# Turning uncentred x and taking its mean off in PSUM, loading q and w2 in smaller parts, and moving the side work to later slots

## The chip, the cores and the metric

Each run uses one core of one Trainium2 chip; the experiments were spread over four chips, each with runs of the kernel before in its own rounds. The metric is the device time of an execution in microseconds (us), the median of several. The kernel before takes 290.69 us (three runs, 290.58 to 290.82). All runs in this study count as fast; there is no slow run among them to set aside. Their mean granted clock of PE still differs a little: nine single executions have 0.991 to 0.994 (one each of e1, e3, e9, e11 and e17, two each of e5 and e12), all others 0.997 or more. Those nine are the slowest of their kernels, by 1.0 to 3.0 us over the mean of the others. What makes the clock dip is not shown; in e5's trace it reads 0.73 from 95 to 100 us, around the end of PE's longest wait there (2.06 us, over at 96.68).

Engines are named as in the profile: PE is TensorE, ACT is ScalarE, DVE is VectorE, POOL is GpSimd; PEld is PE's loading of weights, SP is SyncE. PSUM is the memory in which this kernel accumulates PE's products, SBUF the one in which it keeps its other tiles.

## The reference, cut to what matters

```python
kv  = einsum('bhsd,bhse->bhde', k, v)               # B=8, H=8, S=576, D=64
o   = einsum('bhsd,bhde->bhse', q, kv)
x   = o / sqrt(mean(o*o, -1) + 1e-6) * g_norm       # then [B, S, 512]
xn  = (x - mean(x)) / sqrt(var(x) + 1e-6) * g_ln
out = x + relu(xn @ w1) @ w2                        # 512 -> 2048 -> 512
```

## The kernel before

The rows are worked on in 36 tiles of 128 rows: four per batch, and one tile of remainders for each pair of batches. All large products are bf16 matmuls on PE. Their order is fixed: the w1 matmuls of batch 0, its w2 matmuls, w1 of batch 1, and so on. "mm1" and "mm2" below are those two products.

Everything else (k^T v, q times kv, norms, transposes) is side work that has to be ready before the w1 matmuls of its batch. It is woven into the stream by an agenda. A slot is one w1 group (16 matmuls of 128 columns in batches 0 and 1) or four w2 matmuls. Slots 0 to 15 are w1 of batch 0, 16 to 31 its w2, 32 to 47 w1 of batch 1 (four slots for each tile), and so on. When the program is built, everything registered for a slot is emitted just before that slot's matmuls:

```python
def at(slot, fn): agenda.setdefault(int(slot), []).append((slot, fn))
def tick():
    for _, fn in sorted(agenda.pop(clock[0], []), key=lambda e: e[0]): fn()
    clock[0] += 1

def plan_tile(s, make, turn_at, on_pe):
    at(s, first)           # o on PE; square on ACT; reduction on DVE
    at(s + 2, second)      # root on ACT; inverse, y, x, centred xc on DVE
    at(s + 6, third)       # variance on ACT
    at(turn_at, fourth)    # xc^T: on PE with an ACT copy, or by DMA
```

So a slot number does not delay an instruction in time. It decides where it stands in each engine's queue, and each engine works its queue off in order (e12 below shows it for DVE). The slots that the change moves:

```python
at(20, lambda: (rstd_of(0), t.clear()))
at(14.5, q_start); at(19, q_turns); at(22, lambda: kv_of(1))
for j, s, tn in ((0, 24, 30), (1, 27, 34), (2, 31, 38), (3, 35, 42)):
    plan_tile(s, lambda j=j: main_tile(1, j), tn, True)
at(36, lambda: kv_of(2))
at(36.9, lambda: turn_q_dma(2))      # DVE repacks q of batch 2, then a DMA transposes it
for j, s, tn in ((0, 45, 51), (1, 49, 55), (2, 53, 61), (3, 57.5, 64)):
    plan_tile(s, lambda j=j: main_tile(2, j), tn, False)
# ... likewise for batches 3 to 7 and the remainders
```

The start is done by hand. For batch 0's first tiles, x is formed on DVE in f32, then centred and multiplied by g_ln in two halves, each half transposed on PE and copied to SBUF:

```python
t[0].x_g()                           # x = (o * g_norm) * inv, f32, with its row sum
for c, xc in enumerate(halves_xc(0)):            # xc = (x - mean) * g_ln, bf16, 256 columns
    half_turn(0, c, xc, nc.scalar.copy)          # 2 transposes, 1 copy 128x256
t[1].red(); t[1].x_g()
xc1 = list(halves_xc(1))
# slot 1: the rest of q's turns, turn of tile 1, o of tile 2;  slot 2: x of tile 2
# slot 5: turn of tile 2, o of tile 3
```

mm2 of batch 0 keeps four PSUM accumulators open and runs through w2's rows in three parts, `(0, 8), (8, 12)` for all four tiles, then `12 to 16` tile by tile, each followed by its closing step `finish` on DVE (scale, add x, store).

## Time and profile before

| | before |
|---|---|
| median | 290.69 us (290.58 to 290.82) |
| profiled span | 288.8 us |
| PE busy | 280.9 us, 97% |
| DVE, ACT busy | 149.8 and 153.2 us, 52% and 53% |

From the page of the kernel before, the engine table (busy time, share of the span, instructions) and the row that gives PE's busy share in 40 equal slices, in tenths:

```profile
PE 280.9 (97%) x2295; PEld 157.9 (55%) x2295; DVE 149.8 (52%) x331; ACT 153.2 (53%) x333; POOL 41.0 (14%) x69
PE   7889999999999999999999999999999999999994
```

PE bounds it. Only the first slices have air. The view of waits of the kernel before, for PE (what was waited for: us in total, times, longest), says the same; it leaves out very short waits:

```profile
PE even L225 <- DMA v_in<-in_v_dram: 1.5, 1, 1.5
PE p L198 <- DVE eps_sb L137: 1.2, 1, 1.2
PE tp L554 <- DVE xc L547: 0.4, 1, 0.4
PE p L413 <- DMA xT_blk<-xc: 0.2, 1, 0.2
```

The first two are at the very start (loads of k and v; the first fill matmuls, which do no useful work and are meant to warm PE up). The third is the wait for tile 1's centred x, at 17.30 us. The last is one wait near 112 us. In between, for 95 us, the view has no wait of PE.

The timeline of the kernel before, 14 to 20 us, all engines (start us, us, engine, line, operation, out<-in, count, in brackets the idle time before and its releaser). L554 are the transposes of tiles 0 and 1, L413 the w1 matmuls:

```profile
14.20 0.68 PE L554 MATMUL tp<-identity,xc 128*128 128x128 bf16 x4
14.52 0.77 ACT L555 COPY xT_blk<-tp 128x256 bf16<-128x256 bf16 x2 [1.10 <-PE tp L554]
14.95 1.34 PE L413 MATMUL p<-xT_blk,w_sb 128*128 128x128 bf16 x16
...
17.30 0.29 PE L554 MATMUL tp<-identity,xc 128*128 128x128 bf16 x2 [0.39 <-DVE xc L547]
...
18.05 1.26 PE L413 MATMUL p<-xT_blk,w_sb 128*128 128x128 bf16 x16
```

Tile 0's first w1 group starts at 14.95, tile 1's at 18.05. This stretch is what the change wants to shorten. Now a stretch in the middle, w1 of batch 1, in the same view (PE lines, one DVE line and one POOL line):

```profile
53.96 1.96 PE L413 MATMUL p<-xT_blk,w_sb 128*128 128x128 bf16 x32
55.45 0.82 DVE L203 COPY q_p<-q_in 128x2560 bf16<-128x2560 bf16 x1
55.76 0.39 PE L348 MATMUL tp<-identity,xc 128*128 128x128 bf16 x4
55.98 3.74 PE L413 MATMUL p<-xT_blk,w_sb 128*128 128x128 bf16 x64
...
61.72 0.68 POOL L93 DMA_DIRECT2D k_in<-in_k_dram  x1 [0.31 <-issue]
```

The turn of a tile at 55.76 and 64 w1 matmuls behind it, without a gap. DVE repacks q of batch 2 at 55.45, and when its DMA transpose has landed, POOL may issue the loads of batch 3, at 61.72.

### The profile page before, as it was taken

The page shows a single profiled execution, that of the slowest core. Times are in us where ns is not written, and L with a number is a line of the kernel's source. Part 1 is how long each engine was busy: PE and PEld are TensorE (multiplying, and loading weights), DVE is VectorE, ACT ScalarE, POOL GpSimd, SP SyncE. Part 2 cuts the span into 40 slices and gives each one's busy share as a digit, 9 for nine tenths or more (in the row PEclk, how much of TensorE's full clock was granted, in tenths as well). Part 3 has the DMA queues.
Part 4 walks back from the last instruction along what each step waited for, and adds up shares of the span by engine and source line. Part 5 has one row for each costly group of instructions (what it writes and reads, how often), then busy time and mean ns, then how long its engine had stood idle before and what let it go on. Part 6 is the DMA issues. An engine that isn't in the chain of part 4 may idle for free.

```text
span 288.8 us, 5753 instructions
## 1 busy us (share of the span) xinstructions
PE 280.9 (97%) x2295; PEld 157.9 (55%) x2295; DVE 149.8 (52%) x331; ACT 153.2 (53%) x333; POOL 41.0 (14%) x69
## 2 busy tenths in 40 slices
PE   7889999999999999999999999999999999999994
PEld 3579756995479644444444444444444444444444
DVE  5774119938897783764376935762578200220022
ACT  3477844985379733872288318921893066016400
POOL 8522510041005004100500032000000000000000
PEclk9999999999999999999999999999999999999999
DMA  7999999979788959996994189947203410230033
GB/s 214 199 206 205 198 190 195 214 112 193 138 173 101 194 108 157 202 159 120 157 217 68 39 152 219 155 84 149 56 18 64 101 36 0 48 81 19 0 73 75
DMA packets 67546, 36.76 MB, mean 127 GB/s; under 512 B 35516, under 2 KB 62524, under 8 KB 67520
## 3 DMA queue, kind: packets, MB, share of 16 engines
q0 software_dynamic: 28528, 17.76, 43.8%
q1 hardware_dynamic: 38480, 17.91, 31.2%
q10 hardware_dynamic: 512, 0.72, 0.7%
q8 instruction: 18, 0.29, 0.4%
q14 instruction: 8, 0.07, 0.1%
HBM read 36.71 MB, written 9.44 MB: 160 GB/s over the span
## 4 chain that ended last, share of the span: by engine, by line
PE 85%; DMA 5%; DVE 5%; ACT 2%; issue 1%; SPq 1%; DVEq 0%; POOLq 0%
PE p L413 41%; PE p L429 37%; PE o_ps L271 2%; DMA v_in<-in_v_dram 2%; DMA qt<-q_p 2%; PE kv_ps L246 2%; DMA xT_blk<-xc 1%; DVE ss L298 1%; ACT m L416 1%; DVE x_blk L322 1%; DVE y L303 1%; DVE o_sb L434 1%; PE p L198 1%; SPq L205 1%; ACT rms L308 0%
## 5 line engine op out<-in xcount | busy, mean ns | idle before, releaser
L413 PE MATMUL p<-xT_blk,w_sb 128*128 128x128 bf16 (+2 forms) x1024 | 131.6, 286 | 0.6 <-DMA xT_blk<-xc 0.2
L429 PE MATMUL p<-w_sb,m 128*128 128x512 bf16 (+2 forms) x608 | 129.1, 368 | 0.0
L416 ACT ACTIVATE m<-p 128x512 bf16<-128x512 f32 x144 | 85.2, 596 | 43.0 <-PE p L413 40.5
L413 PEld LDWEIGHTS <-w_sb 128*128 128x128 bf16 x1024 | 78.7, 98 | 44.9 <-issue 1.5
L429 PEld LDWEIGHTS <-m 128*128 128x128 bf16 x608 | 57.0, 98 | 62.0
L434 DVE SCALAR_TENSOR_TENSOR o_sb<-p,rstd,x_blk 128x512 f32<-128x512 f32 (+2 forms) x38 | 27.3, 720 | 52.2 <-PE p L429 41.2
L277 ACT ACTIVATE sq<-o_ps 128x512 f32<-128x512 f32 x35 | 20.9, 596 | 41.7 <-PE o_ps L271 41.7
L298 DVE TENSOR_REDUCE ss<-sq 128x8 f32<-128x512 f32 x35 | 23.7, 678 | 13.0 <-ACT sq L277 12.9
L340 ACT ACTIVATE dev<-x_blk,st_blk 128x512 f32<-128x512 f32 x36 | 25.7, 714 | 6.2 <-DVE st_blk L326 6.1
L332 DVE SCALAR_TENSOR_TENSOR xc<-x_blk,st_blk,g_ln_sb 128x512 bf16<-128x512 f32 x34 | 25.6, 752 | 1.2
L303 DVE TENSOR_TENSOR y<-o_ps,inv 128x512 f32<-128x512 f32 x33 | 22.8, 692 | 3.4 <-PE p L413 0.5
L322 DVE SCALAR_TENSOR_TENSOR x_blk<-y,g_norm_sb 128x512 f32<-128x512 f32 x33 | 22.8, 692 | 1.1
L315 DVE RECIPROCAL inv<-rms 128x8 f32<-128x8 f32 x36 | 7.2, 201 | 23.0 <-ACT rms L308 23.0
L422 DVE RECIPROCAL rstd<-rstd 128x4 f32<-128x4 f32 x9 | 1.6, 175 | 31.2 <-ACT rstd L421 31.1
L308 ACT ACTIVATE rms<-ss,eps_sb 128x8 f32<-128x8 f32 x36 | 10.7, 296 | 11.5 <-DVE ss L298 11.4
L98 POOL COPY gate<-qt 1x1 bf16<-1x1 bf16 x5 | 0.9, 177 | 106.4 <-DMA qt<-q_p 106.4
L271 PEld LDWEIGHTS <-qt 128*128 128x128 bf16 (+1 forms) x156 | 10.2, 100 | 8.1 <-issue 1.7
L271 PE MATMUL o_ps<-kv_pack,qt 128*128 128x128 bf16 (+1 forms) x156 | 13.7, 220 | 0.2
L198 PE MATMUL p<-fill_sb 128*128 128x512 bf16 x27 | 8.0, 448 | 1.2 <-DVE eps_sb L137 1.2
L340 ACT ACTIVATION_READ_ACCUMULATOR dev<-x_blk,st_blk 128x1 f32 x36 | 6.8, 189 | 0.0
L249 ACT CAST kv_pack<-kv_ps 64x256 bf16<-64x256 f32 x7 | 2.6, 366 | 7.7 <-PE kv_ps L246 7.7
L246 PEld LDWEIGHTS <-k_in 128*64 128x64 bf16 x280 | 5.0, 112 | 2.6 <-issue 2.5
(80 smaller groups left out, 110.5 us busy)
## 6 DMA issues: line engine op xcount, KB each, us to landing
out_dram<-o_sb SPq DMA_DIRECT2D x70, 128.0 KB, 2.4
w_sb<-in_moe_w_ch_dram POOLq DMA_DIRECT2D x8, 512.0 KB, 15.2
q_in<-in_q_dram POOLq DMA_DIRECT2D x7, 320.0 KB, 12.3
k_in<-in_k_dram POOLq DMA_DIRECT2D x7, 320.0 KB, 6.0
v_in<-in_v_dram POOLq DMA_DIRECT2D x7, 320.0 KB, 8.6
q_in<-in_q_dram POOLq DMA_DIRECT2D x8, 256.0 KB, 12.3
k_in<-in_k_dram POOLq DMA_DIRECT2D x7, 256.0 KB, 6.7
v_in<-in_v_dram POOLq DMA_DIRECT2D x7, 256.0 KB, 10.6
```

The source lines that it names most:

```text
L198: nc.tensor.matmul(p1, lhsT=fill_sb[:, :128], rhs=fill_sb, start=True, stop=True)
L271: nc.tensor.matmul(flat[rows, hp * 128:(hp + 1) * 128], lhsT=lhsT_of(hp), rhs=kvp[:, hp, :], start=True, stop=True)
L277: nc.scalar.activation(self.sq_t, self.o_ps, func=AF.Square)
L298: nc.vector.tensor_reduce(self.ss, self.sq_t, axis=AX.X, op=ALU.add)
L303: nc.vector.tensor_mul(self.y_t, self.o_ps, self.inv().to_broadcast([128, H, D]))
L322: nc.vector.scalar_tensor_tensor(x_blk[:, ts].rearrange("p (h d) -> p h d", h=H), in0=self.y_t, scalar=1.0, in1=g_norm_sb.to_broadcast([12 ...
L332: nc.vector.scalar_tensor_tensor(self.xc_t, in0=x_blk[:, self.ts], scalar=st[:, 1, self.ts:self.ts + 1], in1=g_ln_sb, op0=ALU.add, op1=ALU ...
L340: nc.scalar.activation(dev, x_blk[:, ts], func=AF.Square, bias=st[:, 1, ts:ts + 1], accum_out=st[:, 2, ts:ts + 1])
L413: nc.tensor.matmul(p1[:, i, :], lhsT=w1_sb[:, kk, de * 128:(de + 1) * 128], rhs=blk[2][:, kk, sl], start=(kk == 0), stop=(kk == nK - 1))
L416: nc.scalar.activation(m1[:, de0:de0 + per, sl], p1, func=AF.Relu)
L429: nc.tensor.matmul(p2[:, c0:c1], lhsT=m1s[b][:, de, ts * 128:(ts + 1) * 128], rhs=w2_sb[:, de, c0:c1], start=(de == 0), stop=(de == nDe - 1))
L434: nc.vector.scalar_tensor_tensor(o_sb[:, c0:c1], in0=p2[:, c0:c1], scalar=rstds[b][:, ts:ts + 1], in1=blks[b][0][:, ts, c0:c1], op0=ALU.mu ...
```

## The change

The intent is to feed PE sooner at the start, then to fit the later work to the new pace. It has three parts:

- **A, the start.** For tiles 0 to 2, x is turned without being centred: x^T is a matmul with the identity, and into the same PSUM accumulator goes ones x diag(-mean), which takes the mean off. g_ln is now a factor per partition, applied in the copies out of PSUM, so it is needed transposed; four small fp32 matmuls make it. The f32 x is formed later. q's upper half is loaded in two parts. Tile 2's o and turn get new slots (2 and 4).
- **W, w2.** Its later quarters are loaded in pieces of two row blocks and used as `(0,8), (8,10), (10,12), (12,14)`, then `14 to 16` tile by tile with the closing steps.
- **S, the slots.** Side work of batches 0 to 4 goes to later slots, mostly by one to two. S1 is the tiles of batch 1, S2 is kv and q of batch 2, S34 is the rest.

```diff
+    def x_b(self):                     # A: x without g_ln, not centred, bf16, with its row sum
+        self.i = self.inv().to_broadcast([128, H, D])
+        ...scalar_tensor_tensor(self.xb, in0=self.og_ps, ..., in1=self.i, accum_out=st[:, 0, ts])
+    def mean_b(self):                  # diag = identity * rowsum * (-1/512)
+    def turn_b(self, split):
+        def turned(kk):  matmul(tps[kk // 2][:, kk % 2], lhsT=xb[kk], rhs=identity, start=True, stop=False)
+        def centred(kk): matmul(tps[kk // 2][:, kk % 2], lhsT=ones_sb, rhs=diag, start=False, stop=True)
+        for kk in range(2 if split else nK):
+            nc.scalar.activation(dst[:, kk], tps[kk // 2][:, kk % 2], func=AF.Copy,
+                                 scale=g_lnT_sb[:, kk:kk + 1])
+        if split:  nc.vector.tensor_mul(dst[:, 2:], tps[1], g_lnT_sb[:, 2:] ...)
     ...
     t[0].o_g(ps2, "p2")
+    for kk in range(nK):               # g_ln transposed, fp32
+        nc.tensor.matmul(glT[:, kk:kk + 1], lhsT=gl_row[:1, kk * 128:(kk + 1) * 128],
+                         rhs=one_sb[:1], start=True, stop=True)
+    nc.vector.tensor_copy(g_lnT_sb, glT)
     dead = fill(3)
     t[1].o(); t[1].sq()
     ...
-    fill(5, dead)
-    t[0].x_g()
-    for c, xc in enumerate(halves_xc(0)): half_turn(0, c, xc, nc.scalar.copy)
-    t[1].red(); t[1].x_g(); xc1 = list(halves_xc(1))
+    fill(6, dead)
+    t[0].x_b(); t[1].red(); t[1].root(); t[0].mean_b(); t[0].turn_b(False)
+    t[1].x_b(); t[1].mean_b()
     # slot 1: turn of tile 1, then q's third turn, then x_g of tiles 0 and 1
     # slot 2: o, sq, red, root, o_g, x_b, mean_b of tile 2
-    at(5, lambda: t[2].turn(True))
+    at(4, before_4)                    # turn_b(True) and x_g of tile 2, then q's fourth turn
 # S1
-for j, s, tn in ((0, 24, 30), (1, 27, 34), (2, 31, 38), (3, 35, 42)):
+for j, s, tn in ((0, 25, 31), (1, 28, 35), (2, 32, 39), (3, 36, 43)):
 # S2
-at(36, lambda: kv_of(2));   at(36.9, lambda: turn_q_dma(2))
+at(37.5, lambda: kv_of(2)); at(38.9, lambda: turn_q_dma(2))
 # S34, cut: q_start 14.5 -> 16.2, q_turns 19 -> 20, kv_of(1) 22 -> 22.5, rstd_of(0) 20 -> 20.3;
 # tiles of batch 2 at 45, 49, 53, 57.5 -> 47, 51, 55, 59.5; rem(1) 62 -> 64;
 # batch 3: load 47 -> 48.5, kv 56 -> 58, tiles from 66 step 5 -> 68 step 4.3;
 # batch 4: load 68 -> 68.5, kv 84 -> 86, tiles from 96 step 5 -> 98.5 step 4.5; rem(3) +3.5;
# q of batches 3 and 4 by 2 and 2.6
 # W
-for de0, de1 in ((0, nDe // 2), (nDe // 2, nDe * 3 // 4)):
+for de0, de1 in ((0, 8), (8, 10), (10, 12), (12, 14)):
```

More of the change, by code (lines that the diff above doesn't have):

```diff
@@ L107, in load_w1, with load_w2 @@
             w1_sb[:, :, sl], moe_w_ch1[:, sl].rearrange("(ko p) n -> p ko n", p=128))
-    def load_w2(c):
-        n = nDe // 4
+    def load_w2(de0, de1):
         nc.gpsimd.dma_start(
-            w2_sb[:, c * n:(c + 1) * n, :],
-            moe_w_ch2[c * n * 128:(c + 1) * n * 128, :].rearrange("(ko p) n -> p ko n", p=128))
+            w2_sb[:, de0:de1, :],
+            moe_w_ch2[de0 * 128:de1 * 128, :].rearrange("(ko p) n -> p ko n", p=128))
     def pairs(t, hp0, hp1):
@@ L122 @@
     gate = consts.tile([1, 1], bf16)
+    ones_sb = consts.tile([128, 128], bf16)
+    one_sb = consts.tile([128, 1], f32)
+    nc.vector.memset(one_sb, 1.0)
+    g_lnT_sb = consts.tile([128, nK], f32)
+    nc.vector.memset(ones_sb, 1.0)
     nc.vector.memset(fill_sb, 0.0)
@@ L131 @@
     make_identity(nc, identity)
-    nc.gpsimd.dma_start(q_in[0][64:, :, :J], up(q, 0))
+    nc.gpsimd.dma_start(q_in[0][64:, :, :2], up(q, 0)[:, :, :2])
     load_w1(1)
     load_w1(2)
+    nc.gpsimd.dma_start(q_in[0][64:, :, 2:J], up(q, 0)[:, :, 2:])
     load_w1(3)
@@ L155 @@
         nc.vector.memset(t, 0.0)
-    load_w2(0)
-    load_w2(1)
+    load_w2(0, 4)
+    load_w2(4, 8)
     for dst, src in ((q_in, q), (k_in, k), (v_in, v)):
         load(dst[1], src, 1)
-    load_w2(2)
-    load_w2(3)
+    for de in range(8, nDe, 2):
+        load_w2(de, de + 2)
     qts, held, blks, rstds, m1s, q_ps = {}, {}, {}, {}, {}, {}
@@ L284, in o_g, with turned, centred @@
                                  rhs=kv_g[:, hp, :], start=True, stop=True)
+        def x_b(self):
+            _, st, _ = self.blk
+            self.i = self.inv().to_broadcast([128, H, D])
+            self.xb = work.tile([128, H, D], bf16, tag="xc", bufs=4, name="xb")
+            nc.vector.scalar_tensor_tensor(
+                self.xb, in0=self.og_ps, scalar=1.0, in1=self.i, op0=ALU.mult, op1=ALU.mult,
+                accum_out=st[:, 0, self.ts:self.ts + 1])
+        def mean_b(self):
+            self.diag = work.tile([128, 128], bf16, tag="diag", name="diag")
+            nc.vector.tensor_scalar(
+                self.diag, identity, scalar1=self.blk[1][:, 0, self.ts:self.ts + 1],
+                scalar2=-1.0 / Dm, op0=ALU.mult, op1=ALU.mult)
+        def turn_b(self, split):
+            ts = self.ts
+            flat = self.xb.rearrange("p h d -> p (h d)")
+            tps = [ps_out.tile([128, 2, 128], f32, tag="ops", name="tp") for _ in range(2)]
+            def turned(kk):
+                nc.tensor.matmul(tps[kk // 2][:, kk % 2], lhsT=flat[:, kk * 128:(kk + 1) * 128],
+                                 rhs=identity, start=True, stop=False)
+            def centred(kk):
+                nc.tensor.matmul(tps[kk // 2][:, kk % 2], lhsT=ones_sb, rhs=self.diag,
+                                 start=False, stop=True)
+            turned(0)
+            turned(2)
+            for kk in range(0, nK, 2):
+                centred(kk)
+                turned(kk + 1)
+                centred(kk + 1)
+            dst = self.blk[2][:, :, ts * 128:(ts + 1) * 128]
+            for kk in range(2 if split else nK):
+                nc.scalar.activation(dst[:, kk], tps[kk // 2][:, kk % 2], func=AF.Copy,
+                                     scale=g_lnT_sb[:, kk:kk + 1])
+            if split:
+                nc.vector.tensor_mul(dst[:, 2:], tps[1],
+                                     g_lnT_sb[:, 2:].rearrange("p (k o) -> p k o", o=1)
+                                     .to_broadcast([128, 2, 128]))
+            del self.xb, self.diag
         def x_g(self):
@@ L288, in x_g @@
             ts = self.ts
-            nc.vector.scalar_tensor_tensor(
-                x_blk[:, ts].rearrange("p (h d) -> p h d", h=H), in0=self.og_ps, scalar=1.0,
-                in1=self.inv().to_broadcast([128, H, D]), op0=ALU.mult, op1=ALU.mult,
-                accum_out=st[:, 0, ts:ts + 1])
+            nc.vector.tensor_mul(
+                x_blk[:, ts].rearrange("p (h d) -> p h d", h=H), self.og_ps, self.i)
             nc.vector.tensor_scalar_mul(st[:, 1, ts:ts + 1], st[:, 0, ts:ts + 1], -1.0 / Dm)
-            del self.og_ps
+            del self.og_ps, self.i
         def red(self):
@@ L426, in mm2_part @@
         for de in range(de0, de1):
-            if de % 4 == 0:
+            if de % 4 == 0 and (b or de < 8 or ts % 2 == 0):
+                tick()
+            elif de % 4 == 2 and b == 0 and de > 8 and ts % 2 == 0:
                 tick()
@@ L482 @@
     nc.vector.stream_shuffle(g_ln_sb, gl_row, [0] * 32)
-    del gl_row
     qts[0] = qt_pool.tile([128, JJ, HP, 128], bf16, tag="qt", name="qt")
@@ L531 @@
     t[0].o_g(ps2, "p2")
+    glT = ps_out.tile([128, nK], f32, tag="ops", name="glT")
+    for kk in range(nK):
+        nc.tensor.matmul(glT[:, kk:kk + 1], lhsT=gl_row[:1, kk * 128:(kk + 1) * 128],
+                         rhs=one_sb[:1], start=True, stop=True)
+    nc.vector.tensor_copy(g_lnT_sb, glT)
+    del glT, gl_row
     dead = fill(3)
@@ L536, with before_2, before_4 @@
     t[1].o_g(ps1, "p1")
-    fill(5, dead)
+    fill(6, dead)
     del dead
-    t[0].x_g()
-    def halves_xc(i):
-        x_blk, st, _ = t[i].blk
-        for c in range(2):
-            cs = slice(c * Dm // 2, (c + 1) * Dm // 2)
-            xc = work.tile([128, Dm // 2], bf16, tag="xch", bufs=4, name="xc")
-            nc.vector.scalar_tensor_tensor(xc, in0=x_blk[:, i, cs], scalar=st[:, 1, i:i + 1],
-                                           in1=g_ln_sb[:, cs], op0=ALU.add, op1=ALU.mult)
-            yield xc
-    def half_turn(i, c, xc, copy):
-        tp = ps_out.tile([128, 2, 128], bf16, tag="ops", name="tp")
-        for kk in range(2):
-            nc.tensor.transpose(tp[:, kk, :], xc[:, kk * 128:(kk + 1) * 128], identity)
-        copy(t[i].blk[2][:, 2 * c:2 * c + 2, i * 128:(i + 1) * 128], tp)
-    for c, xc in enumerate(halves_xc(0)):
-        half_turn(0, c, xc, nc.scalar.copy)
-    t[1].red()
-    t[1].x_g()
-    xc1 = list(halves_xc(1))
+    t[0].x_b()
+    t[1].red()
+    t[1].root()
+    t[0].mean_b()
+    t[0].turn_b(False)
+    t[1].x_b()
+    t[1].mean_b()
     def before_1():
+        t[1].turn_b(True)
         turn_first(2, ps_m, "misc")
-        tp = ps2.tile([128, HP, 128], bf16, tag="p2", name="tp")
-        turn_groups(tp, 3, 0, H)
-        half_turn(1, 0, xc1[0], nc.scalar.copy)
+        t[0].x_g()
+        t[1].x_g()
+    def before_2():
         t[2].o()
-        half_turn(1, 1, xc1[1], nc.vector.tensor_copy)
         t[2].sq()
-        nc.scalar.copy(qts[0][:, 3], tp)
         t[2].red()
         t[2].root()
-        del tp, xc1[:]
-    def before_2():
         t[2].o_g(ps2, "p2")
+        t[2].x_b()
+        t[2].mean_b()
+    def before_4():
+        t[2].turn_b(True)
         t[2].x_g()
-        t[2].xc()
+        turn_first(3, ps_m, "misc")
     def before_5():
@@ L602 @@
         at(16 + i, lambda i=i: t[i].var())
-    at(20, lambda: (rstd_of(0), t.clear()))
+    at(20.3, lambda: (rstd_of(0), t.clear()))
     def q_start():
@@ L617, in q_turns @@
         del q_ps[1]
-    at(14.5, q_start)
-    at(19, q_turns)
-    at(22, lambda: kv_of(1))
-    for j, s, tn in ((0, 24, 30), (1, 27, 34), (2, 31, 38), (3, 35, 42)):
+    at(16.2, q_start)
+    at(20, q_turns)
+    at(22.5, lambda: kv_of(1))
+    for j, s, tn in ((0, 25, 31), (1, 28, 35), (2, 32, 39), (3, 36, 43)):
         plan_tile(s, lambda j=j: main_tile(1, j), tn, True)
     at(46, lambda: rstd_of(1))
-    at(36, lambda: kv_of(2))
-    at(36.9, lambda: turn_q_dma(2))
-    for j, s, tn in ((0, 45, 51), (1, 49, 55), (2, 53, 61), (3, 57.5, 64)):
+    at(37.5, lambda: kv_of(2))
+    at(38.9, lambda: turn_q_dma(2))
+    for j, s, tn in ((0, 47, 53), (1, 51, 57), (2, 55, 62.5), (3, 59.5, 66)):
         plan_tile(s, lambda j=j: main_tile(2, j), tn, False)
-    plan_tile(62, lambda: rem_tile(1), 69, False)
+    plan_tile(64, lambda: rem_tile(1), 71, False)
     at(78, lambda: rstd_of(2))
-    for b in range(3, B):
-        s = 32 * b
-        at(47 if b == 3 else s - 60,
-           lambda b=b: load_batch(b, qts[b - 1][:1, J, HP - 1, 127:],
-                                  *([blks[2][2][:1, nK - 1, 511:]] if b == 4 else [])))
-        d = -41 if b == 3 else -45
-        at(s + d + (1 if b < 5 else 0), lambda b=b: kv_of(b))
-        at(s + d + 1.7, lambda b=b: turn_q_dma(b))
+    for b, at_load, at_kv, at_q, at_o, step in (
+            (3, 48.5, 58, 58.7, 68, 4.3), (4, 68.5, 86, 87.3, 98.5, 4.5),
+            *((b, 32 * b - 60, 32 * b - 45, 32 * b - 43.3, 32 * b - 32, 5) for b in range(5, B))):
+        at(at_load, lambda b=b: load_batch(b, qts[b - 1][:1, J, HP - 1, 127:],
+                                           *([blks[2][2][:1, nK - 1, 511:]] if b == 4 else [])))
+        at(at_kv, lambda b=b: kv_of(b))
+        at(at_q, lambda b=b: turn_q_dma(b))
         for j in range(J):
-            o = s + d + (11 if b == 3 else 13) + 5 * j
+            o = at_o + step * j
             plan_tile(o, lambda b=b, j=j: main_tile(b, j), o + 6, False)
         if b % 2:
-            plan_tile(s - 14, lambda b=b: rem_tile(b), s - 8, False)
-        at(s + 14, lambda b=b: rstd_of(b))
+            o = 32 * b - (10.5 if b == 3 else 14)
+            plan_tile(o, lambda b=b: rem_tile(b), o + 6, False)
+        at(32 * b + 14, lambda b=b: rstd_of(b))
     at(32 * B + 14, lambda: rstd_of("rem"))
@@ L660 @@
         p2s[ts] = None
-        mm2_part(0, ts, p2, nDe * 3 // 4, nDe)
+        mm2_part(0, ts, p2, 14, nDe)
         finish(0, ts, p2)
```

## The prediction

> **What bounds it.** TensorE. The engine table gives PE 97% busy, and the groups by line show no idle time on it after 18 us except 0.2 us before batch 3's first w1 matmul. From 18 us on the stream runs at 56 ns per 128-column matmul (48 in 2.69 us, chain of waits), which is the 55.6 ns that the Trainium skill, "TensorE: Matmul & The Clock Gate", section "Wait — 56ns, not 53.3ns?", states. So only the first 18 us, about 0.5 us between 22 and 33 us (176 matmuls at 58 ns; the chain passes through ScalarE there) and about 0.4 us near 110 us can be won.
>
> **Before, by the timeline.** Tile 0: x ends at 13.43, then mean 0.15, centring by halves 0.88, transposes at 14.20, copies to 15.29, first 16 w1 matmuls end at about 16.1. Tile 1: reduction only at 14.46, x at 15.84, PE idle 0.39 at 17.30, its w1 matmuls end at 19.14. Between 14.2 and 18.4 us PE has about 2.3 us of work: 1.9 lost. Queue 0 moves about 200 KB/us until 31 us; w2's last chunk lands near 45.1 us by the DMA records and is wanted near 45.3.
>
> **Change.** Removed per tile: mean and centring on VectorE before the turn (0.15 + 0.88). Added: a diagonal (estimate 0.15), and x must be formed again in f32 (0.69) later. PE does 8 matmuls for 4 per tile: 12 x 56 ns = 0.67 us. Four copies of 128x128 take about what two of 128x256 took (issue spacing about 0.17 us, estimate from the two squares of tile 0: 0.66 together). The transposed g_ln costs four tiny fp32 matmuls hidden among fills. q's upper half in two parts lets w1's second and third chunks land about 0.65 us sooner (128 KB at 200 KB/us); w2's later halves give their first use about 1.3 us of slack.
>
> **Critical path.** Tile 0 gains nothing: six fills and the diagonal behind tile 1's reduction put its turn at 14.3 and its first group's end at 16.1 to 16.3. Tile 1 gains: x at 14.9, mean at 15.9, so at 16.3 its turn waits for nothing; its w1 group ends near 18.1, 1.0 us sooner. But 0.8 us of that is work moved later (turn of q's last part 0.35, tile 2's o 0.22, its longer turn 0.22). And tile 2's o now stands two w1 groups (1.8 us) ahead of its turn, while its chain square, reduction, root, inverse, x took 3.1 us before: I expect PE to wait 0.5 to 1.1 us there, at about 20.5. The second w1 chunk's first PSUM tile also waits for tile 1's f32 x. Against this, later slots that suit an earlier PE should remove the 0.4 us near 110 and part of the 0.5 us. Sum: between -1.0 and +0.9; the retuned slots (batches 1 to 3 one to two slots later) speak for an earlier PE, so I lean to a small gain.
>
> **Predicted** 290.3 us, 8 in 10 within 289.4 to 291.3. Faster by over 2%: 0.01; within 2%: 0.98; slower: 0.01.
>
> **What would show it.** Timeline: tile 0's first w1 group ends within 0.3 us of before; tile 1's near 18.1; an idle gap on PE before tile 2's turn; w1 matmuls of the second chunk not waiting for DMA; start of mm2 of batch 0 (before 32.98) within 1 us; no wait on w2. Stretches after 120 us unchanged in PE time.
>
> **What would make it wrong.** fp32 matmuls that take over 0.3 us each would delay tile 1's o and VectorE's copy ahead of tile 0's x. Tile 2 not waiting would give 289.3. Batch 1's v (lands near 37.5, wanted at 38.7) or q's DMA transpose (lands near 46.7) could become the wait if PE runs ahead, and give the gain back.

## More of the kernel before

The view by stretches of the kernel before (stretch in us, its length, then busy us and instructions of PE, PEld, DVE, ACT, POOL, the granted clock, the DMA share, GB/s), for w1 of batch 1 and for everything from w1 of batch 3 on:

```profile
49.00:65.40 16.40, 16.40 (x319) 16.16 (x317) 10.46 (x22) 14.10 (x33) 3.86 (x7) 1.00 0.89 168
...
112.20:289.00 176.80, 172.82 (x996) 82.49 (x995) 77.27 (x162) 84.93 (x180) 12.64 (x21) 1.00 0.56 96
```

In w1 of batch 1 PE is busy for all 16.40 us, and ACT, which only serves it, for 14.10. A stretch in which two engines are this full has little room for a side step that comes late.

## The result, and the profile after

| | before | after |
|---|---|---|
| median, same rounds | 290.63 us | 299.66 us (299.11 to 300.0, four runs) |
| ratio | | 1.031 (95% interval 1.0291 to 1.0326) |
| profiled span | 288.8 us | 297.4 us |
| PE busy | 280.9 us, 97% | 281.9 us, 95% |

A ratio, here and below, is the mean time of one kernel's runs over that of the other's runs of the same rounds, so it is not quite the ratio of the medians beside it. The kernel is 9.0 us slower, far outside the predicted range.

The same two rows of the page, kernel after:

```profile
PE 281.9 (95%) x2291; PEld 160.1 (54%) x2316; DVE 150.5 (51%) x336; ACT 153.7 (52%) x337; POOL 43.0 (14%) x72
PE   7898999798999899999999999999999999999994
```

PE's recorded busy time grew by 1.0 us, but this trace lacks 25 matmul records (2291 for 2316 weight loads; before has all 2295), so the true growth is larger: the traces of e6, e7 and e11 below, which have all or nearly all of the new start, all 2316 records and the full clock, show 283.5 to 284.3 us, some 3 us above before (first fills that took up to 1.3 us longer, see e7, are part of it). The view of waits has 5.9 us more than before's (9.2 against 3.3, summed from the lines here and there). So about two thirds of the 8.6 us by which the span grew are new waiting; the rest would be more work on PE. The row of slices has digits under 9 at places where before had none, in the first half of the run only. The view of waits of the kernel after, for PE:

```profile
PE p L461 <- DMA xT_blk<-xc: 1.9, 2, 1.4
PE p L461 <- ACT xT_blk L398: 1.4, 3, 0.6
PE p L203 <- DVE eps_sb L142: 1.4, 1, 1.4
PE p L461 <- DVE o_sb L484: 1.2, 1, 1.2
PE even L230 <- DMA v_in<-in_v_dram: 1.0, 1, 1.0
PE tp L312 <- DVE xb L296: 1.0, 1, 1.0
PE o_ps L276 <- DMA qt<-q_p: 1.0, 1, 1.0
...
PE p L461 <- ACT xT_blk L327: 0.3, 1, 0.3
```

Five of these are new (ACT copies under two lines, the closing step, tile 2's x, the transposed q), and the wait for x^T by DMA has grown from 0.2 to 1.9 us. To place them, the starts of the phases on PE, read from the two timelines (us):

| first matmul of | before | after | difference |
|---|---|---|---|
| w2 of batch 0 | 32.98 | 35.77 | +2.8 |
| w1 of batch 1 | 49.09 | 51.82 | +2.7 |
| w2 of batch 1 | 65.36 | 72.74 | +7.4 |
| w1 of batch 2 | 81.15 | 88.93 | +7.8 |
| w2 of batch 2 | 96.01 | 105.55 | +9.5 |
| w1 of batch 3 | 112.25 | 120.60 | +8.4 |
| end of the span | 288.8 | 297.4 | +8.6 |

The loss has two large pieces: 2.8 us before w2 of batch 0, and 4.7 us within w1 of batch 1. About one more is lost in batch 2, and from w1 of batch 3 on nothing to speak of is: 176.6 us to the end of the span before, 176.8 after. So does the view by stretches of the kernel after show it, for w1 of batch 1 and for the end:

```profile
52.00:73.00 21.00, 17.32 (x318) 16.34 (x317) 11.55 (x25) 15.21 (x33) 1.29 (x3) 1.00 0.56 96
...
121.00:298.00 177.00, 171.44 (x982) 82.49 (x997) 77.65 (x162) 84.85 (x180) 12.06 (x20) 1.00 0.57 94
```

In w1 of batch 1 PE does the same work in 21.00 us instead of 16.40, with nearly 4 us idle. The DMA share fell too (0.56 from 0.89): the loads of batch 3 did not run here.

**The start.** Timeline of the kernel after, 11 to 24 us, PE lines and one of ACT. L583 makes the transposed g_ln, L312 are transposes, L327 the copies that apply g_ln, L461 the w1 matmuls:

```profile
11.55 1.05 PE L583 MATMUL glT<-one_sb,gl_row 1*128 1x1 f32 x8
...
15.27 0.28 PE L312 MATMUL tp<-identity,xb 128*128 128x128 bf16 x2
...
15.75 1.14 ACT L327 ACTIVATE xT_blk<-tp,g_lnT_sb 128x128 bf16<-128x128 f32 x4 [0.50 <-PE tp L316]
16.17 1.66 PE L461 MATMUL p<-xT_blk,w_sb 128*128 128x128 bf16 x16 [0.29 <-ACT xT_blk L327]
17.67 0.27 PE L312 MATMUL tp<-identity,xb 128*128 128x128 bf16 x2
18.77 1.25 PE L461 MATMUL p<-xT_blk,w_sb 128*128 128x128 bf16 x16
...
23.30 0.29 PE L312 MATMUL tp<-identity,xb 128*128 128x128 bf16 x2 [1.04 <-DVE xb L296]
```

Four fp32 matmuls of one output column each are eight records and 1.05 us, and they stand ahead of tile 1's o, whose start moves from 12.14 to 13.18. Behind that o come six fills, and the chain of waits leads through all six into tile 0's turn, at 15.27 (before 14.20). Its four copies take 1.14 us where the two of before took 0.77. Tile 0's first w1 group starts at 16.17 and tile 1's at 18.77; before it was 14.95 and 18.05. The gap of 1.04 us before tile 2's turn was predicted.

**w1 of batch 1.** Timeline of the kernel after, 54 to 72 us, PE, DVE and POOL. L398 on ACT (named in the brackets) is the copy of a transposed tile, L484 the closing step of mm2, L208 the repacking of q:

```profile
53.25 2.72 DVE L484 SCALAR_TENSOR_TENSOR o_sb<-p,rstd,x_blk 128x512 f32<-128x512 f32 x4
54.05 1.95 PE L461 MATMUL p<-xT_blk,w_sb 128*128 128x128 bf16 x32 [1.18 <-DVE o_sb L484]
...
57.91 1.05 PE L461 MATMUL p<-xT_blk,w_sb 128*128 128x128 bf16 x16 [0.57 <-ACT xT_blk L398]
...
63.25 2.84 PE L461 MATMUL p<-xT_blk,w_sb 128*128 128x128 bf16 x48 [0.52 <-ACT xT_blk L398]
...
64.89 0.82 DVE L208 COPY q_p<-q_in 128x2560 bf16<-128x2560 bf16 x1
...
67.54 2.84 PE L461 MATMUL p<-xT_blk,w_sb 128*128 128x128 bf16 x48 [0.34 <-ACT xT_blk L398]
71.39 0.40 PE L276 MATMUL o_ps<-kv_pack,qt 128*128 128x128 bf16 x4 [1.01 <-DMA qt<-q_p]
...
71.89 0.68 POOL L93 DMA_DIRECT2D k_in<-in_k_dram  x1 [0.31 <-PE o_ps L276]
```

Three causes can be read here:

- Four closings of batch 0's mm2 stand in one run on DVE, 53.25 to 55.97, and PE waits 1.18 us for the PSUM that they hold. It takes W and S1 together: the runs below with W and the old S1 (e2, e4, e5, e9) have the closings in two pairs and a wait of 0.34 or 0.35 us, e6 with W and the new S1 has all four in one run and 1.18 again, and e16 with S1 alone has no such wait.
- Before the first w1 group of tiles 1, 2 and 3 PE waits for the ACT copy of that tile's x^T: 0.57, 0.52, 0.34 (S1). The turns are now one group ahead of their use; before, they were two ahead (slots 30, 34, 38, 42 for tiles that start at 32, 36, 40, 44).
- DVE repacks q of batch 2 at 64.89, in before at 55.45. Its transpose lands so late that PE waits 1.01 us, and the loads of batch 3 start 10.2 us later than before, 71.89 for 61.72 (S2). In batch 2 that comes back: DVE waits 2.16 us at 86 us for q of batch 3, and the x^T of batch 2 come late, which is the wait of 1.9 us at the head of the list. (With S2 undone, in e6 below, that wait is gone from the list. It takes S34 as well: e3 and e5, which have both, show 2.5 and 2.1 us of it, e12 with S2 alone 0.3, e13 with S34 alone none.)

### The profile page after: what moved, and what is told of

It reads as the page before. It is cut to its first block, busy times and chain, and to the rows that moved or that the text cites. A ratio compares the mean times of both kernels' runs of the same rounds, so it can differ in the third digit from the quotient of the medians.

```text
span 297.4 us, 5785 instructions
## 1 busy us (share of the span) xinstructions
PE 281.9 (95%) x2291; PEld 160.1 (54%) x2316; DVE 150.5 (51%) x336; ACT 153.7 (52%) x337; POOL 43.0 (14%) x72
## 4 chain that ended last, share of the span: by engine, by line
PE 76%; DMA 9%; DVE 6%; ACT 2%; issue 2%; SPq 1%; POOL 1%; DVEq 0%; POOLq 0%
PE p L461 35%; PE p L479 35%; DMA q_in<-in_q_dram 4%; DMA v_in<-in_v_dram 2%; PE o_ps L276 2%; DMA qt<-q_p 2%; PE kv_ps L251 2%; DMA xT_blk<-xc 1%; DVE o_sb L484 1%; DVE ss L346 1%; DVE x_blk L370 1%; DVE y L351 1%; PE p L203 1%; ACT m L464 1%; DVE xc L380 1%
## 5 line engine op out<-in xcount | busy, mean ns | idle before, releaser
L461 PE MATMUL p<-xT_blk,w_sb 128*128 128x128 bf16 (+2 forms) x1016 | 131.9, 285 | 5.6 <-DMA xT_blk<-xc 1.9
L479 PE MATMUL p<-w_sb,m 128*128 128x512 bf16 (+2 forms) x592 | 126.5, 368 | 1.5 <-issue 1.0
L461 PEld LDWEIGHTS <-w_sb 128*128 128x128 bf16 x1024 | 78.8, 98 | 49.9 <-issue 4.3
L484 DVE SCALAR_TENSOR_TENSOR o_sb<-p,rstd,x_blk 128x512 f32<-128x512 f32 (+2 forms) x38 | 27.1, 720 | 50.6 <-PE p L479 45.0
L380 DVE SCALAR_TENSOR_TENSOR xc<-x_blk,st_blk,g_ln_sb 128x512 bf16<-128x512 f32 x33 | 24.8, 752 | 1.2
```

The costliest lines, as they stand in the source:

```text
L380: nc.vector.scalar_tensor_tensor(self.xc_t, in0=x_blk[:, self.ts], scalar=st[:, 1, self.ts:self.ts + 1], in1=g_ln_sb, op0=ALU.add, op1=ALU ...
L461: nc.tensor.matmul(p1[:, i, :], lhsT=w1_sb[:, kk, de * 128:(de + 1) * 128], rhs=blk[2][:, kk, sl], start=(kk == 0), stop=(kk == nK - 1))
L479: nc.tensor.matmul(p2[:, c0:c1], lhsT=m1s[b][:, de, ts * 128:(ts + 1) * 128], rhs=w2_sb[:, de, c0:c1], start=(de == 0), stop=(de == nDe - 1))
L484: nc.vector.scalar_tensor_tensor(o_sb[:, c0:c1], in0=p2[:, c0:c1], scalar=rstds[b][:, ts:ts + 1], in1=blks[b][0][:, ts, c0:c1], op0=ALU.mu ...
```

## The experiments

The theory from the traces: A costs about 3 us at the start, W about 1, and S the rest, since the later slots take away the lead that side work needs. The rival, which the prediction believed in: the slots suit a PE that is early, and hurt only because the start came late; without A, S would be harmless, and with a mended A it would help. Each compares with runs of the kernel before in the same rounds, 290.46 to 290.71 us.

| run | edit | median us (range) | ratio, 95% interval |
|---|---|---|---|
| e1_start_only | before + A | 294.79 (294.27 to 295.65) | 1.0143, 1.0119 to 1.0166 |
| e2_w2_halves_only | before + W | 291.42 (291.19 to 291.51) | 1.0025, 1.0008 to 1.0042 |
| e3_slots_only | before + S | 298.41 (297.68 to 300.61) | 1.0277, 1.0233 to 1.032 |
| e4_start_and_w2 | before + A + W | 294.92 (294.34 to 295.38) | 1.0143, 1.0123 to 1.0163 |
| e5_turn_slots_back | after, S1 undone | 298.60 (296.41 to 299.92) | 1.0264, 1.0209 to 1.032 |
| e6_q2_slots_back | after, S2 undone | 296.51 (296.37 to 297.12) | 1.0204, 1.0189 to 1.0219 |
| e7_gl_early | e4, g_ln turned earlier | 295.01 (294.78 to 295.28) | 1.0149, 1.0134 to 1.0164 |
| e8_gl_early_turn2_late | e7, turn of tile 2 a slot later | 292.99 (292.52 to 293.11) | 1.0075, 1.0058 to 1.0092 |
| e9_both_slots_back | after, S1 and S2 undone | 293.89 (293.54 to 295.32) | 1.012, 1.0087 to 1.0153 |
| e10_w2_close_in_fours | e2, last quarter of w2 whole | 290.81 (290.51 to 291.07) | 1.0004, 0.999 to 1.0019 |
| e11_turn2_late_only | e4, turn of tile 2 a slot later | 294.17 (293.71 to 295.31) | 1.0126, 1.01 to 1.0152 |
| e12_q2_slots_on_before | before + S2 | 295.01 (294.13 to 296.08) | 1.0151, 1.0119 to 1.0182 |
| e13_later_slots_on_before | before + S34 | 289.69 (289.59 to 290.12) | 0.9975, 0.9963 to 0.9987 |
| e14_repairs_together | A and W mended, S34 | 291.36 (290.42 to 291.68) | 1.0021, 1.0007 to 1.0035 |
| e15_tile0_copies_shared | e14, tile 0's copies on two engines | 290.59 (290.15 to 291.26) | 1.0005, 0.9993 to 1.0016 |
| e16_turn_slots_on_before | before + S1 | 293.46 (293.27 to 293.94) | 1.0107, 1.0092 to 1.0121 |
| e17_four_fillers_fewer | e15, 14 fills for 18 | 290.64 (290.27 to 291.95) | 1.0009, 0.9993 to 1.0025 |

All of them give the reference's result.

### The three parts alone (e1, e2, e3) and A with W (e4)

e1 is before with the part marked A of the diff, e2 with the part W, e3 with all the lines of S. e4 is after with all the lines of S as they were before.

> The new start alone (uncentred turns, diagonal, g_ln turned by fp32 matmuls, q's upper half in two parts), with the slots and the w2 use of before. Theory 1 (the start costs what mm2 of batch 0 began late by in the changed kernel, 35.77 against 32.98 us, and hands on no more): 293.2 to 293.8 us, mm2 of batch 0 begins 2.6 to 3.0 us late, no waits of over 0.3 us on PE after 40 us. Rival (a late start by itself upsets batches 1 and 2, whatever the slots): 297 us or more.

> Only w2's later chunks loaded and used in halves. Theory 1 (harmless by itself but for the four closings of batch 0's tiles, which fall within 1.7 us and wait for VectorE): 290.7 to 292.0 us, a PE wait for o_sb of up to 1.2 us before the first w1 matmuls of batch 1. Rival 2 (the closings in one burst put VectorE behind and that is what costs batches 1 and 2 their 6 us): 294 us or more.

> Only the retuned slots of batches 1 to 4. Theory 1 (turns of batch 1 stand one slot before their use, q of batch 2 is repacked two slots later and so batch 3's loads are late): 294 to 297 us, three PE waits of about 0.5 us for copies of x turned in batch 1. Rival 2: within 0.5 us of before. Rival 3 (the slots suit an early PE and harm only together with the late start): 290 to 291 us.

> The whole change but for the retuned slots. Theory 1: 293.3 to 295 us, that is 5 to 6 us under the changed kernel. Rival 2: 298 us or more, as the changed kernel.

Measured: A +4.3 us, W +0.9, S +7.9, A with W +4.4. A and S cost 1.0 and 1.4 us more than the ranges of theory 1 allowed. The rival falls with e3: on the untouched start, with the PE exactly as early as before, the new slots alone cost nearly as much as the whole change. The view of waits of e3, PE, has the same kinds of wait as the kernel after:

```profile
PE o_ps L271 <- DMA qt<-q_p: 2.6, 2, 2.1
PE p L413 <- DMA xT_blk<-xc: 2.5, 1, 2.5
PE p L413 <- ACT xT_blk L350: 2.2, 3, 1.4
```

That is 7.3 us together, for q's transpose, the x^T by DMA and the ACT copies of x^T. Before has 0.2 of the second and none of the others. The parts do not add up. 4.3 + 0.9 + 7.9 is 13.1, and the change costs 9.0; on top of A and W, S costs 4.7 us (299.66 less 294.92). So the slots as a whole hurt less on the late start, by 3.2 us, but they do not help. The waits show where the difference lies, not why: q's transpose takes 1.0 us in after for 2.6 in e3, the ACT copies 1.4 for 2.2, and a wait of 0.83 us for v at 105 us, which e4 has, is gone in after.

In e1 the one profiled execution was the slowest of its four and ran with a granted clock of 0.76 and 0.90 between 10 and 20 us, so sizes are not read from that trace. e4's trace, at full granted clock, puts mm2 of batch 0 at 35.94, against 32.98 before: the start costs 3.0 us of its 4.4 there. The rest are later waits of PE in that trace: 0.35 for a closing, 0.73 for x^T at 93 us and the 0.83 for v.

e2's small loss has a place. Timeline of e2, PE, the second w1 group of batch 1:

```profile
50.37 1.05 PE L412 MATMUL p<-xT_blk,w_sb 128*128 128x128 bf16 x16 [0.34 <-DVE o_sb L435]
```

It waits for the closing step of mm2, as in the kernel after, though for 0.34 us instead of 1.18.

### The slots, undone on after (e5, e6, e9)

```diff
 # e5                                        # e6
-((0, 25, 31), (1, 28, 35), ...)            -at(37.5, kv_of(2)); at(38.9, turn_q_dma(2))
+((0, 24, 30), (1, 27, 34), ...)            +at(36, kv_of(2));   at(36.9, turn_q_dma(2))
 # e9: both
```

> The changed kernel with the slots of batch 1's four tiles alone put back (24/30, 27/34, 31/38, 35/42 in place of 25/31, 28/35, 32/39, 36/43), so that a turn again stands two w1 groups ahead of its use. Theory 1a (the turns one group before their use are what costs): the three waits for copies (1.4 us in the changed kernel) go, mm2 of batch 1 begins 1.5 to 3 us sooner than 72.74, time 296.5 to 298 us. Rival 1b (it is the later repacking of batch 2's q): within 0.7 us of the changed kernel, 299 to 300 us.

> The changed kernel with only batch 2's k-v product and q repacking put back (slots 36 and 36.9 in place of 37.5 and 38.9). Rival 1b: the 1.0 us wait for the transposed q goes, batch 3's loads are issued several us sooner than 71.9, waits for xT of batch 2 go: 296.5 to 298 us. Theory 1a: 298.8 to 300 us.

> The changed kernel with both e5's and e6's slots put back; the new slots of batch 2's tiles and of batches 3 and 4 stay. If those two groups hold all that the slots cost: 294.5 to 295.4 us, as e4 (294.92). If batch 2's and later slots cost too: 296 us or more. If they help: 294 us or less.

e6 gives back 3.15 us, e9 5.8 us. e5 gives back 1.1 us by the medians, but its four runs are spread over 3.5 us (296.41 to 299.92), so by itself it decides nothing. The two at 299.8 and 299.9 are those with a clock of 0.994; the other two (296.41 and 297.44) lie 2.7 us under the kernel after. With S2 undone as well (e6 against e9) undoing S1 is worth 2.6, which agrees. e9 ends 1.0 us under e4, which has the same start and w2 and all of the old slots: what is left of S, the part S34, is a small gain. That was not expected when S had looked like one thing.

### The slots, each group alone on before (e12, e13, e16)

```diff
 # e12: S2 alone     +at(37.5, kv_of(2)); at(38.9, turn_q_dma(2))
 # e16: S1 alone     +((0, 25, 31), (1, 28, 35), (2, 32, 39), (3, 36, 43))
 # e13: S34 alone, every other moved slot of the diff
```

> The kernel before with only batch 2's k-v product and q repacking moved to the new slots (37.5 and 38.9). In before, the copy that repacks q ran at 55.45, ahead of tile 3's last steps; behind them it would run near 59.4, its transpose land near 65, and the first product of batch 2 at 62.45 wait some 2.5 us: 292.5 to 295 us. If the slots harm only together with the others: 290.5 to 291.2 us.

> The kernel before with only batch 1's four tiles in the new slots. Theory 1a: waits of 0.3 to 0.5 us for copies of x at three turns and batch 2's repacking pushed back by tile 3: 292 to 295 us. If the turns are harmless by themselves: 290.5 to 291.2 us.

> The kernel before with all the new slots but batch 1's tiles and batch 2's k-v product and q. If the later slots help by themselves as e9 suggests (1.0 us under e4): 289.8 to 290.4 us, which would beat both kernels. If they only help a late PE: 290.5 to 291.2 us.

S2 +4.3 us, S1 +3.0, S34 -0.8; together 6.5 of the 7.9 that they cost in one. (Two of e12's four runs have a low clock; the other two give S2 +3.6.) Timeline of e12, one DVE line and one of PE:

```profile
58.46 0.82 DVE L203 COPY q_p<-q_in 128x2560 bf16<-128x2560 bf16 x1
...
65.99 0.40 PE L271 MATMUL o_ps<-kv_pack,qt 128*128 128x128 bf16 x4 [2.66 <-DMA qt<-q_p]
```

The repacking moved from 55.45 to 58.46. Its line names no wait, so its input was not what held it. In slot order it now stands behind tile 3's second step (slot 37: inverse, y, x, centring), while 36.9 stands ahead of it; DVE does that first, and the centring ends at 58.5. The Trainium skill, "PSUM — Partial Sum Buffer", section "Engine vs sequencer instructions", calls the queues of ScalarE, VectorE and GpSimd strict FIFO, and this trace agrees: the copy starts as soon as tile 3's centring is off the engine. 3.0 us later on DVE became a wait of 2.66 us on PE, since tile 0 of batch 2 takes its q from that transpose. A second wait in e12, 0.66 us, is of another kind: the pool that the kernel calls `ps_m` has one PSUM buffer, k^T v of batch 2 (now in slot 37) and the turns on PE share it, and tile 2's turn in slot 38 waits until ACT has copied k^T v out.

The view of waits of e16, the two lines with a releaser that before does not have:

```profile
PE kv_ps L246 <- ACT xT_blk L350: 1.4, 1, 1.4
PE p L413 <- ACT xT_blk L350: 0.9, 2, 0.5
```

Together 2.3 us for ACT copies, of the 3.0 that e16 loses. The 1.4 is not a w1 group that wants its x^T: it is k^T v of batch 2, in slot 36, that wants the one buffer of `ps_m`, which tile 1's turn, moved to slot 35, still holds. In the kernel after, k^T v has moved on to slot 37 and this wait is absent, so e16 has a wait that is no part of the whole change; there S1 shows as 1.4 us of waits for copies before w1 groups and 0.8 us more for the closings. As for the 0.9, the copy itself takes 0.58 us, as before. What makes it late is the ACT queue ahead of it: in the kernel after, ahead of the copy that ends at 63.2, ACT works from 61.24 on through a square, a root and a ReLU, and PE's group wants the copy at 62.7. One group of w1 is 0.9 us long. A lead of two groups covered such a queue here, a lead of one did not.

e13 is the version that beats both kernels, the one before by 0.8 us. In its view of waits nothing is left after the start but stops of 0.2 us without a releaser (such stops stand only in traces that lack matmul records, here 25 of 2295, so they are probably not real); the wait for x^T at 112 us is gone, and w1 of batch 3 starts at 111.09 instead of 112.25 (0.2 us of that is a small product now done behind it). So the observation in the prediction was right that there was something to win near 110 us by moving slots.

### The start, repaired piece by piece (e7, e8, e11)

```diff
 # e7: the four g_ln matmuls and their copy moved from behind t[0].o_g to right behind fill(18)
 # e11, on e4                                 # e8: the same, on e7
-at(4, turn_b and x_g of tile 2, q's fourth turn)
+at(4, q's fourth turn); at(5, turn_b and x_g of tile 2)
```

> The change but for its slots (e4), with the four fp32 matmuls that turn g_ln and their copy moved ahead of the first k-v product, where PE idles for the load of v. If the 1.05 us that they took in front of tile 1 was on the path: mm2 of batch 0 begins 0.7 to 1.1 us sooner than in e4 (35.94), time 293.8 to 294.3 us. If the wait before tile 2's turn takes it back: no sooner, 294.6 to 295.2 us.

> e7 with tile 2's turn one w1 group later (slot 5 in place of 4, q's last turn stays at 4). If the 1.0 us wait before tile 2's turn was a loss: a further 0.6 to 1.0 us, mm2 of batch 0 at 34.0 to 34.5, time 292.8 to 293.6 us, the wait for xb under 0.2 us. Rival: the wait only moves to the first w1 matmuls of tile 2, time as e7.

> e4 with only tile 2's turn moved one w1 group later. If the wait before the turn was a plain loss of its 1.0 us: 293.6 to 294.2 us. e8 was 2.0 us under e7; if that holds here: 292.7 to 293.3 us, and moving g_ln's turn is worth nothing by itself.

e7 missed: no gain. e8 gained 2.0 us over e7, yet the same edit in e11 gains 0.75 over e4 (the wait of 1.04 us for tile 2's x is gone there, but in the two traces one for v near 105 us has grown from 0.83 to 1.42 us). The first fills explain part of it. Timelines of e7, then e8, PE, the 18 first fills and the g_ln matmuls behind them:

```profile
1.38 6.87 PE L203 MATMUL p<-fill_sb 128*128 128x512 bf16 x18 [1.38 <-DVE eps_sb L142]
8.18 1.05 PE L539 MATMUL glT<-one_sb,gl_row 1*128 1x1 f32 x8
```

```profile
1.38 5.61 PE L203 MATMUL p<-fill_sb 128*128 128x512 bf16 x18 [1.38 <-DVE eps_sb L142]
7.02 1.02 PE L539 MATMUL glT<-one_sb,gl_row 1*128 1x1 f32 x8
```

The same 18 matmuls took 6.87 us in one profiled execution and 5.61 in the other. The Trainium skill, "TensorE: Matmul & The Clock Gate", section "What's actually happening", describes it: the array runs at half clock until a free-running window of about 3.4 us has found it busy, and where that window falls varies from run to run. Here the g_ln matmuls follow the fills, so k^T v of batch 0 started 0.9 us later in e7 (9.15 against 8.21). In the trace of e7 the g_ln matmuls were thus moved off the path behind k^T v only to lie on the path ahead of it; e7 also keeps the wait of 1.04 us before tile 2's turn, which e8 does not have. Whether this is the whole of e7's miss is not settled: the other three executions of e7, of which there is no trace, were all within 0.5 us of each other, so a random window would have had to fall alike four times. By e4 to e7 the early g_ln is worth nothing, by e11 to e8 (294.17 to 292.99) 1.2 us.

### w2 and the sum of the repairs (e10, e14, e15, e17)

```diff
 # e10, on e2
-for de0, de1 in ((0, 8), (8, 10), (10, 12), (12, 14)):    ... mm2_part(0, ts, p2, 14, 16); finish
+for de0, de1 in ((0, 8), (8, 10), (10, 12)):              ... mm2_part(0, ts, p2, 12, 16); finish
 # e14: e8 with e10's w2, and S34
 # e15, on e14                                # e17, on e15
-t[0].turn_b(False)                           -fill(18)
+t[0].turn_b(True)   # half the copies on DVE +fill(14)
```

> e2 with the last quarter of w2 used in one piece again for each tile (12 to 16), so that the four closings of batch 0 stand 0.86 us apart, as before, in place of 0.43; loads still in halves. If the burst of closings is what e2 lost 0.9 us to: 290.4 to 290.9 us and no wait for o_sb on PE. If it is the smaller loads: 291.2 to 291.6 us.

> The change with the repairs of e8, e9 and e10 together: g_ln turned early, tile 2's turn one group later, batch 0 closed in fours, batch 1's tiles and batch 2's k-v product and q in their old slots. If the parts add up: 292.99 less 0.6 (e10) less 1.0 (e9): 291.2 to 291.8 us. If not, 292.5 us or more.

> e14 with tile 0's copies shared as the other tiles' are, two on ScalarE and one of double width on VectorE, in place of four on ScalarE (1.14 us in the changed kernel, against 0.77 for two of double width before). If those copies hold PE up at tile 0: mm2 of batch 0 begins 0.3 to 0.6 us sooner than in e14 and the time falls by as much. If VectorE's delay of tile 1 takes it back: as e14.

> e15 with 14 fillers in place of 18 ahead of the early g_ln matmuls. If the fillers' length (they run at half speed until some moment between 5 and 7.5 us that differs by run) is what delays the k-v product behind g_ln's turn: the first k-v matmul at 8.2 to 8.5 in place of 8.87, the spread of the runs under 0.6 us, median 290.0 to 290.3 us. If fewer fillers leave the clock cold later: 290.6 us or more.

e10 removes W's loss: 290.81, no difference from before that can be told, and no wait for a closing step. On DVE its closing steps start at 46.57, then two from 49.77 on, and one at 51.68, as in before (46.54, 49.74, 51.66); in e2 all four lie between 49.57 and 52.9. So it was the bunching of the closings that cost, and loading w2 in smaller pieces, which e10 keeps, is worth nothing.

e14 adds the repairs up about as foretold. e15, which lets DVE do half of tile 0's copies, is 0.8 us lower by the medians and 0.5 by the means, with ranges that overlap; in the traces its mm2 of batch 0 starts 0.5 us sooner (33.52 for 33.99). e17 missed its time, though not its step: in its trace the first k^T v matmul stands at 8.27, as foretold, and mm2 of batch 0 starts at 32.99, but the median is that of e15. Its spread is one run at a clock of 0.992 (291.95); the other five lie within 0.7 us, e15's six within 1.1, too few to tell apart. With everything mended the kernel is level with before (1.0005), but it includes S34, and S34 without A and W (e13) is 289.69 us. On the same chip and in the same rounds the mended start and w2 are thus 0.9 us behind the old ones. In e15's trace mm2 of batch 0 starts at 33.52, in e13's at 32.83.

## Why the prediction was wrong

The prediction was 290.3 us, within 289.4 to 291.3. It was 299.66.

**The step that failed most:** "the retuned slots (batches 1 to 3 one to two slots later) speak for an earlier PE, so I lean to a small gain." This took the choice of slots as evidence about PE's pace, and put no cost on it. It was 7.9 us by itself (e3), and 4.7 on top of the late start. Two of its costs stood in the code and could have been counted from the trace of before: the turns go from two w1 groups ahead of their use to one, 0.9 us, while an ACT copy of 0.58 us has a queue of ReLU, square and root before it; and slot 38.9 puts q's repacking behind tile 3's second step (slot 38, by then) in DVE's queue, where 36.9 stood ahead of it (slot 37). e12 and e16 show the two at +4.3 and +3.0 us, each with a collision over the one `ps_m` buffer in it (0.7 and 1.4 us). The gain near 110 us that the sentence counted on exists (e13, -0.8).

**The start, mis-sized in four terms.** The sum said between -1.0 and +0.9; e1 and e4 show +4.3 and +4.4.

- "The transposed g_ln costs four tiny fp32 matmuls hidden among fills": they took 1.05 us and pushed tile 1's o from 12.14 to 13.18, since they stand ahead of it on PE, and they were added to the fills, not put in the place of some. The prediction's own list of what could make it wrong had this, for "over 0.3 us each"; 0.26 us each was enough.
- "Four copies of 128x128 take about what two of 128x256 took (issue spacing about 0.17 us)": 1.14 us against 0.77, a spacing of 0.26 ((1.14 - 0.366) / 3, with 0.366 the mean of one). The 0.17 was taken from instructions without a per-partition operand. The Trainium skill, "ScalarE: Activation LUTs", section "What ACT_TABLE_LOAD costs", has 186 ns + 0.833 ns per element, about 93 ns more for each such operand, and about 93 ns of overlap. An estimate from these figures is 386 ns for one of 128 elements, and 293 from start to start. The trace has 366 and 258, nearer to that than to the prediction's 0.17.
- "its first group's end at 16.1 to 16.3": that group started at 16.17 and ended near 17.7, because its turn stands behind six fills that follow tile 1's late o and start at 13.98 instead of 12.93; without the fills, its diagonal (ready at 15.1, behind tile 1's reduction at 14.24) would have held it nearly as long.
- "its w1 group ends near 18.1, 1.0 us sooner": tile 1's ended at 19.86, 0.7 later than before. "Start of mm2 of batch 0 within 1 us" was +2.8.

**w2** was said to get slack from its halves; nothing waited for w2 before or after, and the finer split bunched the closings, +0.9 us (e2; e10 takes it away), and with S1 more so.

**What was right:** the wait before tile 2's turn (0.5 to 1.1 us foretold, 1.04 measured; e11 shows it to be worth 0.75), no wait for w1's or w2's loads, and unchanged stretches after 120 us. And PE bounds the kernel, at the pace that was cited; this is just why a late side step anywhere in the first 120 us shows in the total.

**What stays open:** why S costs 3.2 us less on the late start than on the early one; what the remaining 0.9 us between the mended start and the old one is made of (PE has more to do: 282.9 us busy in e8 against 280.9 in before, with all records in both and first fills of 5.6 us in both, but which of it lies on the path is not shown); what makes the clock dip in single runs of e5, e12 and others; and the spread of e14 and e15 (290.42 to 291.68 in e14), which have the full clock; the length of the first fills is a candidate that e17 does not settle.

## What to carry to other kernels

In a stream that is full on its main engine, a slot of side work has a price: count from the trace what stands ahead of it in its own engine's queue, what shares its PSUM buffer and how much main work is left until it is needed, and treat a moved slot as a change to be costed, not as a hint about what its author saw. A lead of one group of matmuls was too short here and two were enough. And when a change has several parts, run each alone: the part that helped here, by 0.8 us, was hidden inside the part that hurt most.

## What the Trainium skill lacked or had wrong

- "TensorE: Matmul & The Clock Gate", section "Back-to-back issue gap", gives about 81 ns (128 columns) and 131 ns (512 columns) per matmul for streams of weight load and matmul in real kernels. This kernel's stream ran at 56 ns and 216 ns (48 w1 matmuls in 2.69 us, 64 w2 matmuls in 13.81 us, kernel before), the values that the page calls isolated, and that its section "Wait — 56ns, not 53.3ns?" measures.
- The same page has no cost for small fp32 matmuls. Four with one output column each were recorded as eight and took 1.05 us in all.
- The half clock at the start that the page's section "What's actually happening" describes shows in the durations (18 fills in 6.87 or 5.61 us), but the granted clock in the profile read 1.00 over those same microseconds, so this view does not show it. The page's section "Seeing it yourself" warns only in general that clock events in a trace can be unreliable.
- "ScalarE: Activation LUTs", section "What ACT_TABLE_LOAD costs": the estimate from its figures for a copy with a per-partition scale, 386 ns and 293 ns from start to start, was a little high for bf16 out of f32 PSUM: 366 and 258.
